# Splitting the last head group of an attention and long-convolution kernel by queries, and moving key blocks and query weights

## The chip, the core and the metric

The kernel runs on one core of a Trainium2 chip. Its engines are TensorE (PE, with its weight loads shown apart as PEld), VectorE (DVE), ScalarE (ACT), GpSimd (POOL) and SyncE (SP, which here only issues DMAs). The metric is the device time of one execution in microseconds, as the median of several runs. The profile is of one further execution; its times count from the start of its span.

## What is computed

The sequence has 2048 positions and 640 features. Two branches are mixed by a gate per position:

```
g = sigmoid((x * gate_w).sum(-1))                     # x is A_q, (2048, 640)
a = A_q * (causal_long_conv(shift(k) * v, ssm_k) + shift(k) * v * ssm_D)
q = x @ wq, 32 heads of 20;  k = x @ wk, v = x @ wv   # one key and value head for all
p = softmax(q k^T / sqrt(20)) ;  b = (p v) @ wo
out = g * a + (1 - g) * b
```

`shift` is a 4-tap filter along the sequence, and the long convolution is written with Fourier transforms. The softmax is over 2048 keys for 32 heads and 2048 queries: 134 million exponentials, which is most of the work.

## The kernel before

**Attention.** A head group is four heads times 512 queries. There are 32 groups G: four query blocks I of 512 queries with 8 groups each. The four heads sit in four strips of 32 rows, so that four score matmuls (32 rows deep) or four PV matmuls (32 columns wide) can use the array side by side. A tile is (G, j, r): group, block j of 128 keys, head r. A score tile is 128 keys by 512 queries and fills one PSUM bank.

**The score ring.** `stream` lines the tiles up and deals them into units of three and two tiles, in turn. `QK` writes a unit of three to banks 0 to 2 and one of two to banks 3 and 4; `EXP` (L1200) takes the exponential of a unit in one ScalarE instruction of 1536 or 1024 columns, into ETA or ETB; `PV` (L1241) then multiplies by the values and adds up over the key blocks in bank 6. Row 20 of the padded heads carries a bound that stands in for the maximum, and column 20 of the values is one, so that bank 6 also holds the sums. Banks 5 and 7 are left for everything else.

**Tiles on VectorE.** For the pairs (G, j) in `DVE_J` two of the four heads don't go through the ring: `DEXP` computes their exponential by a polynomial on VectorE (L1230, L1233, L1234, L1236). 94 such pairs take 188 of the 2048 tiles.

**A planner.** The instructions on each engine are not in the order of the program text. `Scheduler` plays the whole graph with costs and priorities written into the code and writes out a fixed order for each engine. PE follows the stream of score and PV matmuls, and between them it fits groups of side work (projections, shift filter, convolution, output), each into a free bank from the group's list; where nothing fits it may run filler matmuls on zeros (L1629). Each engine runs its list in order, waiting on semaphores. A changed cost, bank list or priority thus can move instructions anywhere.

**The start.** The transposed input xT is made on PE (L998). The key projection `kproj` makes four groups of 512 keys (L1017), evacuated as kT4 (L1069, L1071); the first block of 128 keys has an evacuation of its own on ScalarE. `weights2` clears the padded query weights `wq_pad` by a GpSimd memset (L983) and copies the heads into it (L986). `qproj` (L1085 and after) makes qT for some groups, squares it, sums the squares by a matmul (L1108), turns the sums into the bound (`cr`, L1114) and writes the bound into row 20 of qT by a DMA ("crow"). `kshift` loads the taps and k (a transposing DMA) and v, makes the diagonal filter matrices `kdiag` on VectorE (L1413), and runs the shift as matmuls (L1424).

**The end.** For G up to 30 `norm` copies bank 6 out, sends the sums through DRAM to spread the reciprocals, and multiplies on GpSimd (L1315). In the last query block the result goes to oT3, and `part` (L1340, L1343) adds up groups 0 to 5 of the output product ahead of time. `tail` does the last group: after its last PV it transposes bank 6 in 32x32 blocks, takes the reciprocal, multiplies, transposes back (L1353 to L1358), adds groups 6 and 7 of the output product (L1363, with warm-up matmuls L1372 beside it), and evacuates (L1387) and stores four row blocks of 128 queries.

Of the kernel before, what the change touches and what calls it, by code (L numbers as in the profile page):

```python
# [7 lines left out]
ALU = mybir.AluOpType  # L8
# [13 lines left out]
LATX = 0.12  # L22
CEX = 0.0633
LATM = {("dve", "dve"): 0.3}
# [145 lines left out]
class Scheduler:  # L170
# [278 lines left out]
    def place(self, op, e):  # L449
# [45 lines left out]
        if e == "pe":  # L495
            if op.name != "qk":
                self.rows = set()
            elif op.cont:
                self.rows.add(op.row)
            else:  # L500
                self.rows = {op.row}
        if op.name == "pv":
            self.can_fill = not op.last
            self.acc = None
        elif op.name == "acc":
            self.acc = op
# [120 lines left out]
DVE_J = [(6,), (), (4, 10), (4, 11), (2, 7, 10), (1, 4, 9, 13), (9,), (2, 7, 12), (3, 8, 13), (2, 6, 10, 14), (3, 9), (1, 4, 8, 12), (1, 2, 7, 10, 13), (8,), (1, 6, 11), (2, 7, 13), (2, 6, 10, 14), (2, 4, 7, 10, 13), (2, 6, 10, 14), (2, 9), (8,), (2, 5, 8, 11, 14), (), (2, 5, 8, 11, 14), (1, 4, 7, 10, 13), (6,), (1, 4, 7, 10, 13), (5,), (1, 4, 8, 12), (2, 5, 10, 11, 14), (1, 10, 11), (2, 8, 13)]  # L627
# [28 lines left out]
class Kernel:  # L656
# [322 lines left out]
    def weights2(self):  # L979
# [3 lines left out]
        self.pool(lambda e: e.memset(T["wq_pad"][:, :, 128:1024].bitcast(I32), 0), (), [("wq_pad", 1)], 2.1, prio=-4,  # L983
                  after=self.crow0 + [self.g.writer["kT4", 0, 128]])
        for lo, hi in ((4, 8), (8, 16), (16, 24), (24, 32)):
            self.pool(lambda e, lo=lo, hi=hi: e.tensor_copy(dst[:, :, lo:hi, 0:20], src[:, :, lo:hi, :]),  # L986
                      [("wqst", 1)], [("wq_pad", 1)], 0.75 if hi - lo == 4 else 1.5, prio=-4, name="wq_cp")
# [21 lines left out]
    def kproj(self):  # L1009
# [3 lines left out]
        for b in range(NB):  # L1013
            gr = self.group("kT", (1.9 if b == 0 else 4.0) + 0.1 * b, banks=(5, 7) if b == 0 else (7, 4, 5))
# [62 lines left out]
    def qproj(self, I, gs, prio, banks, ng):  # L1077
# [4 lines left out]
        for gl, gi in enumerate(gs):  # L1082
            gr = self.group("qp", prio, banks=banks)
            for dc in range(NDC):
# [4 lines left out]
                if dc == 0:  # L1089

                    o.deps.update(self.crow0 or ())
                    if self.crow0:
                        o.deps.add(self.g.writer["mcol"])
                    o.deps.update(self.g.readers.get(("qT", par, gi), ()))
            self.evac(gr, "dve", None, ["qup"], [("qT", par, gi)], 0.7,
# [6 lines left out]
                     [("qT", par, gi)], [("sq", gl)], c_fast(512), prio=-1500.0 if I == 0 and gs[0] == 0 else prio - 500, port=True,  # L1102
# [4 lines left out]
        for gl in range(nq):  # L1107
# [10 lines left out]
                 writes=[("qT", par, gi) for gi in gs], nbytes=4 * nq * 1024, prio=pr, name="crow", lat=1.7)  # L1118
# [15 lines left out]
    def stream(self):  # L1134
# [4 lines left out]
        for G in range(8 * NB):  # L1139
            for j in range(NSC):  # L1140
                mine = order
                if j in DVE_J[G]:
# [12 lines left out]
    def attention(self):  # L1155
# [10 lines left out]
        def score(e, bk, G, j, r):  # L1166
            return e.matmul(self.bank(bk), T["kT4"][32 * r:32 * r + 32, 128 * j:128 * j + 128],  # L1167
                            T[f"qT{G // 8 % 2}"][32 * r:32 * r + 32, G % 8, :], start=True, stop=True,
# [5 lines left out]
        def QK(n):  # L1174
            un = units[n]
            I = un[-1][0] // 8
# [8 lines left out]
            for k, (G, j, r) in enumerate(un):  # L1185
                bk = base[n % 2] + k
                o = op("pe", lambda e, bk=bk, G=G, j=j, r=r: score(e, bk, G, j, r),
                       [self.kkey(j), ("qT", G // 8 % 2, G % 8)], [("ps", bk)], 0.003 if k < len(un) - 1 else 0.216,
                       name="qk", main=True, cont=(k > 0), banks=(bk,))
                o.row = r  # L1190
                o.unit = n
                if k == 0:
# [11 lines left out]
        def DEXP(G, j):  # L1204
# [10 lines left out]
            for h, r in enumerate(rs):  # L1215
# [5 lines left out]
                self.mm(gr, lambda e, bk, r=r: score(e, bk, G, j, r), [self.kkey(j), ("qT", G // 8 % 2, G % 8)],  # L1221
# [17 lines left out]
        def PVmm(r, j, src, key, late=False, **k):  # L1239
            va = "vneg" if late else "vaug"  # L1240
            return op("pe", lambda e: e.matmul(  # L1241
                self.bank(6)[32 * r:32 * r + 32, :], T[va][:, j, :], src,
                start=(j == 0), stop=(j == NSC - 1), tile_position=(0, 32 * r)),
                [key, va, ("vaugb", j // 4)], [] if late else [("ps", 6)], name="pv", **k)

        def PV(G, j, rs, more=False):
            for k, r in enumerate(rs):
# [441 lines left out]
```

## Time and profile before

| | us |
|---|---|
| median of 3 runs (lowest to highest) | 875.41 (875.38 to 875.6) |
| the profiled execution, its own time | 876.13 |
| span of the profiled execution | 874.3 |
| start of the first exponential | 20.80 |
| last exponential begins, ends | 863.68, 864.94 |

PE's granted clock was full (1.00) in nearly the whole span. Busy time by engine over four stretches (us of the span, length, busy us and number of instructions of PE, PEld, DVE, ACT and POOL, granted clock, DMA share, GB/s):

```
24.00:50.00 26.00, 24.86 (x251) 9.70 (x252) 16.10 (x24) 25.72 (x23) 15.17 (x21) 1.00 0.72 156
300.00:600.00 300.00, 296.22 (x2717) 121.04 (x2717) 247.15 (x297) 300.00 (x266) 143.63 (x126) 1.00 0.08 24
840.00:865.00 25.00, 24.73 (x206) 10.14 (x200) 9.46 (x18) 24.93 (x23) 1.27 (x1) 1.00 0.14 45
865.00:874.30 9.30, 4.51 (x36) 2.74 (x36) 5.94 (x9) 0.00 (x0) 0.00 (x0) 0.99 0.21 73
```

How to read the profile: a row of a timeline has the start, the length, the engine, the line of the kernel, the operation, the tile written and the tile read, the count, and in brackets how long the engine was idle before it and who released it. On ScalarE an instruction's length takes in the time it stands in the engine behind its predecessor, so lengths of neighbours overlap; the pace is the distance between starts. SPq and ACTq are the issue of a DMA, not its transfer.

### The profile page before, as it was taken

To read this page: it belongs to the slowest core of one execution; us is meant where nothing else is said; L and a number is where in the kernel's file an instruction comes from. 1 tells how busy PE (TensorE), PEld (TensorE's weight loads), DVE (VectorE), ACT (ScalarE), POOL (GpSimd) and SP (SyncE) were. 2 spreads that over 40 slices of the span, in tenths; PEclk is the share of its full clock that TensorE was granted. 3 is DMA by queue.
4 is the path that set the end of the run, shared out by engine and by line. 5 is a ranking of instruction groups with operands and counts; after the bars stand their busy time and mean duration, and the time that the engine had idled before them with its cause. 6 is when DMAs were issued, how large, how long until landed. Compare 5 with 4: busy or idle time off the path is not lost.

```text
span 874.3 us, 18639 instructions
## 1 busy us (share of the span) xinstructions
PE 854.7 (98%) x8054; PEld 351.3 (40%) x8054; DVE 703.0 (80%) x906; ACT 853.4 (98%) x765; POOL 368.8 (42%) x351
## 2 busy tenths in 40 slices
PE   8999999999999999999999999999999999999997
PEld 5334424444344334444334344444444433243333
DVE  7668988895887888888789888788668788898854
ACT  6999999999999999999999999999999999999995
POOL 3572001357564434653516654436761537410000
PEclk9999999999999999999999999999999999999999
DMA  6900010001100000100000102000100000040211
GB/s 193 210 16 8 20 44 15 20 11 28 33 19 15 19 8 21 44 19 20 13 13 15 45 20 57 21 4 18 44 20 20 13 7 10 13 111 29 58 67 39
DMA packets 49713, 30.71 MB, mean 35 GB/s; under 512 B 32477, under 2 KB 45662, under 8 KB 49630
## 3 DMA queue, kind: packets, MB, share of 16 engines
q1 hardware_dynamic: 48910, 29.13, 12.3%
q8 instruction: 63, 1.03, 0.5%
q10 hardware_dynamic: 720, 0.38, 0.2%
q14 instruction: 20, 0.16, 0.1%
HBM read 17.85 MB, written 6.02 MB: 27 GB/s over the span
## 4 chain that ended last, share of the span: by engine, by line
ACT 93%; PE 6%; DVE 1%; DVEq 0%; POOL 0%; issue 0%; POOLq 0%
ACT ETA L1200 55%; ACT ETB L1200 38%; PE ps L1167 1%; PE ps L1634 1%; PE ps L998 1%; PE ps L1241 1%; PE ps L1085 1%; PE ps L1424 1%; PE ps L1629 0%; PE ps L1017 0%; PE ps L1363 0%; PE ps L1025 0%; DVE outsb L1387 0%; PE ps L1372 0%; DVE IndG L920 0%; PE ps L1108 0%
## 5 line engine op out<-in xcount | busy, mean ns | idle before, releaser
L1200 ACT ACTIVATE ETA<-ps 128x1536 bf16<-128x1536 f32 x372 | 604.7, 1625 | 2.3 <-PE ps L1167 2.3
L1200 ACT ACTIVATE ETB<-ps 128x1024 bf16<-128x1024 f32 x372 | 447.8, 1204 | 1.6 <-PE ps L1167 1.6
L1167 PE MATMUL ps<-qT,kT 32*128 32x512 bf16 x2048 | 298.6, 384 | 11.8 <-ACT ETA L1200 6.4
L1514 POOL TENSOR_TENSOR Pp<-X,K 128x512 f32<-128x512 bf16 x120 | 154.7, 1301 | 169.4 <-DVE K L1502 56.8
L1230 DVE TENSOR_SCALAR dW<-ps 128x512 f32<-128x512 f32 x188 | 129.0, 687 | 79.1 <-PE ps L1167 78.0
L1167 PEld LDWEIGHTS ps<-qT,kT 32*128 32x128 bf16 x2048 | 73.8, 91 | 249.2 <-ACT ETB L1200 126.4
L1241 PE MATMUL ps<-ETA,vaug 128*32 128x512 bf16 x1116 | 151.5, 385 | 0.3 <-ACT ETB L1200 0.3
L1241 PE MATMUL ps<-ETB,vaug 128*32 128x512 bf16 x744 | 146.9, 385 | 0.0
L1236 DVE SCALAR_TENSOR_TENSOR ETd<-dX,dW 128x1024 int16<-128x1024 f32 x94 | 133.8, 1423 | 9.7 <-PE ps L1241 9.5
L1233 DVE SCALAR_TENSOR_TENSOR dX<-dW 128x1024 f32<-128x1024 uint16 x94 | 131.3, 1397 | 1.1
L1234 DVE SCALAR_TENSOR_TENSOR dX<-dX,dW 128x1024 f32<-128x1024 f32 x94 | 126.9, 1350 | 0.4
L1514 POOL TENSOR_TENSOR AB<-Pp 128x256 bf16<-128x256 f32 x80 | 63.2, 790 | 74.4 <-DVE dX L1234 29.8
L1481 PE MATMUL ps<-ssm_kT,Tcs 128*128 128x256 bf16 x600 | 89.4, 274 | 0.0
L1547 PE MATMUL ps<-AB,Tcs 128*128 128x256 bf16 x600 | 88.5, 274 | 0.0
L1629 PE MATMUL ps<-Tcs,zeros 128*32 128x512 bf16 x1072 | 88.4, 385 | 0.1
L1481 PE MATMUL ps<-kv,Tcs 128*128 128x256 bf16 x600 | 87.5, 275 | 0.0
L1514 POOL TENSOR_TENSOR Pp<-Pp 128x512 f32<-128x512 f32 x40 | 56.8, 1419 | 40.9 <-DVE dX L1234 18.2
L1315 POOL TENSOR_TENSOR oTn<-acc,rbc 128x512 bf16<-128x512 f32 x24 | 38.2, 1593 | 76.3 <-DVE dX L1234 32.8
L1481 PEld LDWEIGHTS ps<-kv,Tcs 128*128 128x128 bf16 x600 | 49.9, 98 | 35.7 <-issue 28.7
L1547 PEld LDWEIGHTS ps<-AB,Tcs 128*128 128x128 bf16 x600 | 51.5, 98 | 31.4 <-issue 26.1
L1481 PEld LDWEIGHTS ps<-ssm_kT,Tcs 128*128 128x128 bf16 x600 | 51.0, 98 | 30.6 <-issue 23.7
L1315 POOL TENSOR_TENSOR oT<-acc,rbc 128x512 bf16<-128x512 f32 x7 | 12.1, 1733 | 81.2 <-DMA rbc<-scr_d 46.4
(132 smaller groups left out, 648.3 us busy)
## 6 DMA issues: line engine op xcount, KB each, us to landing
rbc<-scr_d SPq DMA_DIRECT2D x31, 256.0 KB
scr_o<-oTn SPq DMA_DIRECT2D x24, 128.0 KB, 1.7
xn<-in_A_q_dram SPq DMA_DIRECT2D x4, 640.0 KB, 7.7
kv<-in_A_v_dram SPq DMA_DIRECT2D x4, 640.0 KB
out_dram<-outsb SPq DMA_DIRECT2D x14, 160.0 KB, 2.2
oTp<-scr_o SPq DMA_DIRECT2D x12, 160.0 KB, 7.5
wog<-in_B_wo_dram SPq DMA_DIRECT2D x4, 200.0 KB
wo<-in_B_wo_dram SPq DMA_DIRECT2D x4, 200.0 KB, 3.3
```

The lines of the kernel that those rows point to most:

```text
L1167: return e.matmul(self.bank(bk), T["kT4"][32 * r:32 * r + 32, 128 * j:128 * j + 128], T[f"qT{G // 8 % 2}"][32 * r:32 * r + 32, G % 8, :], ...
L1200: op("act", lambda e: e.activation(et(n)[:, 0:w], self.ps[:, lo:lo + w], ACT.Exp, scale=SCALE), [("ps", base[n % 2] + k) for k in range(le ...
L1230: self.evac(gr, "dve", lambda e, bk, h=h: e.tensor_scalar(W[:, 512 * h:512 * h + 512], self.bank(bk), SCALE * LOG2E * 128.0, 128.0 * (127 ...
L1233: V(lambda e: e.scalar_tensor_tensor(X[:, :], w, DP, w, ALU.add, ALU.mult), [kW], ["dX"], c_ps(1024), **k)
L1234: V(lambda e: e.scalar_tensor_tensor(X[:, :], X[:, :], DQ, w, ALU.add, ALU.mult), [kW], ["dX"], c_ps(1024), **k)
L1236: V(lambda e: e.scalar_tensor_tensor(T[f"ETd{pe}"][:, :].bitcast(dt.int16), X[:, :], DA, W[:, :], ALU.mult, ALU.add), [kW, "dX"], [("ETd", ...
L1241: return op("pe", lambda e: e.matmul(self.bank(6)[32 * r:32 * r + 32, :], T[va][:, j, :], src, start=(j == 0), stop=(j == NSC - 1), tile_p ...
L1315: self.pool(lambda e: e.tensor_tensor(out, T["acc"][:, :], T["rbc"][:, :], ALU.mult), ["acc", "rbc"], [key], c_pool(512), prio=p, port=Tru ...
L1481: self.mm(gr, lambda e, bk, lhs=lhs, rhs=rhs, comp=comp, n=n: e.matmul(self.bank(bk, 256, 256 * comp), lhs, rhs, start=(n == 0), stop=(n = ...
L1514: f = lambda e: e.tensor_tensor(out, a, b, alu)
L1547: self.mm(gr, lambda e, bk, lhs=lhs, fc=fc, comp=comp, h=h: e.matmul(self.bank(bk, 256, 256 * h), lhs, AB[:, fc, :, comp, :], start=(fc == ...
L1629: sch.filler = [[lambda e, r=r, st=st: e.matmul(self.bank(6)[32 * r:32 * r + 32, :], self.T["zeros"][:, 0:32], self.T["Tcos"][:, 0, 0:512] ...
```

## The change

1. **The last head group in three parts.** Group 31 is worked in three passes over all keys: queries 0 to 255 (PV into bank 6), 256 to 383 (bank 5) and 384 to 511 (bank 6 again). A ring tile stays 512 columns wide: with 256 queries it holds two key blocks, with 128 queries four, each by a matmul of its own (`split`). The PV matmuls are split in the same way. After each part a new function `tail_o` does the transposes and the normalisation for that part, and the output product of the finished row blocks (three of the four) is done as side work, evacuated in halves of 320 columns and stored while the stream runs. Only the last row block is left for `tail`. The lists of banks of the late side groups take in bank 6.
2. **No VectorE tiles in the last group**, and `DVE_J` dealt out anew: 94 entries before and after, of which the two of group 31 are not used. The first two groups have none.
3. **Key blocks out of the score ring**: the groups of `kproj` may use banks 5 and 7; before, three of the four could also use bank 4.
4. **Query weights first**: the memset of `wq_pad` moves from behind the first crow DMA to behind the copies into wk4; the four copies come after the last key block; `kdiag` waits for the second of them.
5. Bookkeeping: the planner's delay from GpSimd to GpSimd, names of the qT tiles for the fences, fillers for the new banks.

In the order of instructions that the planner makes of it, the first transposes of the third input block go ahead of the first query projection, the first load of v goes ahead of the taps on SP, and the loads of the taps and of k follow.

The core of the diff:

```diff
-LATM = {("dve", "dve"): 0.3}
+LATM = {("dve", "dve"): 0.3, ("pool", "pool"): 0.0}
...
+LASTG = 31
+STAGES = ((0, 256, 6), (256, 128, 5), (384, 128, 6))
...
-        self.pool(lambda e: e.memset(T["wq_pad"][:, :, 128:1024].bitcast(I32), 0), (), [("wq_pad", 1)], 2.1, prio=-4,
-                  after=self.crow0 + [self.g.writer["kT4", 0, 128]])
+        self.pool(lambda e: e.memset(T["wq_pad"][:, :, 128:1024].bitcast(I32), 0), (), [("wq_pad", 1)], 2.0, prio=-8.9,
+                  after=[self.g.writer["wk4"]])
+        self.wq_cp = []
         for lo, hi in ((4, 8), (8, 16), (16, 24), (24, 32)):
...
+                      after=self.crow0 + [self.g.writer["kT4", NB - 1, 0]]))
...
-            gr = self.group("kT", (1.9 if b == 0 else 4.0) + 0.1 * b, banks=(5, 7) if b == 0 else (7, 4, 5))
+            gr = self.group("kT", (1.9 if b == 0 else 4.0) + 0.1 * b, banks=(5, 7))
...
-        for G in range(8 * NB):
-            for j in range(NSC):
+        for G in range(LASTG + len(STAGES)):
+            for j in range(NSC if G < LASTG else NSC * STAGES[G - LASTG][1] // 512):
                 mine = order
-                if j in DVE_J[G]:
+                if G < LASTG and j in DVE_J[G]:
...
+        def score(e, bk, G, j, r, t=0):
+            k, g = qkey(G)
+            m = split(G)
+            n, q0, jt = 512 // m, STAGES[G - LASTG][0] if m > 1 else 0, m * j + t
+            return e.matmul(self.bank(bk, n, n * t), T["kT4"][32 * r:32 * r + 32, 128 * jt:128 * jt + 128],
+                            T[k][32 * r:32 * r + 32, g, q0:q0 + n], start=True, stop=True,
                             tile_position=(32 * r, 0))
...
+                if LASTG <= G < LASTG + len(STAGES) - 1 and j == NSC // split(G) - 1:
+                    self.tail_o(G - LASTG)
...
+    def tail_o(self, h):
+        T = self.T
+        g = 7
+        q0, w, b = STAGES[h]
...
+        o = self.dve(lambda e: e.transpose(acc, self.bank(b, w)), [("ps", b)], [k["acc"]], c_ps(w), prio=p, name="tp%d" % h,
+                     after=[self.tp0] if h else ())
...
+        self.dve(lambda e: e.reciprocal(rcp, v(T["acc"])[:, :, 20]), [k["acc"]], [k["rcp"]], 0.3, prio=p, name="rcp")
+        self.dve(lambda e: e.tensor_tensor(v(T["oTn"]), v(T["acc"]), rcp.unsqueeze(2).to_broadcast([128, w // 32, 32]),
+                                           ALU.mult), [k["acc"], k["rcp"]], [k["oTn"]], c_ps(w), prio=p, port=True,
+                 name="onorm")
+        self.dve(lambda e: e.transpose(T["oT3"][:, g, q0:q0 + w], oTn), [k["oTn"]], [("oT3", g, h)],
+                 c_ps(w), prio=p, name="tp")
...
+        for ci in range(fin[0]):
...
+                gr = self.group("op2s", -800.0 + ci, banks=(7, 6, 5))
+                for g in (6, 7):
+                    self.mm(gr, lambda e, bk, g=g, ci=ci, half=half: self.tail_mm(e, self.bank(bk, HD), ci, half, g),
+                            [("oT3", g) if g < 7 else ("oT3", 7, h_of[ci]), "wog", ("part", ci)], c_mm(HD))
...
+            store(ci)
+
+        self.tail_o(len(STAGES) - 1)
...
-            ["ident", "wtap"], ["kdiag"], c_ps(2560), prio=16, port=True, name="ksh", after=[self.g.writer["kT4", NB - 1, 0]])
+            ["ident", "wtap"], ["kdiag"], c_ps(2560), prio=16, port=True, name="ksh", after=[self.g.writer["kT4", NB - 1, 0], self.wq_cp[1]])
```

## What was predicted, before the changed kernel had run

> **What bounds the kernel now.** I read the page first (busy time by engine, and the chain that ended last), then the waits of ScalarE, then the ScalarE timeline, then the stretches around each wait.
>
> From the page, sections 1 and 4, and one row of section 5:
>
> ```profile
> PE 854.7 (98%) x8054; PEld 351.3 (40%) x8054; DVE 703.0 (80%) x906; ACT 853.4 (98%) x765; POOL 368.8 (42%) x351
> ...
> ACT 93%; PE 6%; DVE 1%; DVEq 0%; POOL 0%; issue 0%; POOLq 0%
> ...
> L1200 ACT ACTIVATE ETA<-ps 128x1536 bf16<-128x1536 f32 x372 | 604.7, 1625 | 2.3 <-PE ps L1167 2.3
> ```
>
> PE shows 98% too, but part of that is filler (L1629, L1634). The chain is 93% exponentials (L1200), so ScalarE sets the time. The durations 1625 and 1204 ns include queueing. The pace is the distance from start to start in the ScalarE timeline: median 1.33 us for a 1536-wide exponential and 0.91 for a 1024-wide one, a pair in 2.24, so about 0.87 ns a column.
>
> The waits of ScalarE (us in total, times, longest), and where they lie in its timeline:
>
> ```profile
> ACT ETA L1200 <- PE ps L1167: 2.3, 2, 1.4
> ...
> ACT ETB L1200 <- PE ps L1167: 1.6, 1, 1.6
> ```
>
> ```profile
> 20.80 1.45 ACT L1200 ACTIVATE ETA<-ps 128x1536 bf16<-128x1536 f32 x1 [0.92 <-PE ps L1167]
> 23.84 1.02 ACT L1200 ACTIVATE ETB<-ps 128x1024 bf16<-128x1024 f32 x1 [1.59 <-PE ps L1167]
> ...
> 51.11 1.45 ACT L1200 ACTIVATE ETA<-ps 128x1536 bf16<-128x1536 f32 x1 [1.40 <-PE ps L1167]
> ```
>
> From 20.8 us to the last exponential's end at 864.94 there are only two real holes, 1.59 and 1.40 us. A change can win in four places: the prologue before 20.8, these holes, the number of exponential columns, and the 9.36 us from 864.94 to the end of the span, 874.30.
>
> **Hole 1, 22.2 to 23.8.** The second score unit (banks 3 and 4) starts only at 23.38. One key-block group had been put into bank 4, and its evacuation runs 22.35 to 23.30. It is late because VectorE stood still beside a GpSimd memset (timeline, VectorE and GpSimd):
>
> ```profile
> 21.31 1.97 POOL L983 MEMSET wq_pad<- 128x2240 int32 x1 [1.80 <-DVE IndG L920]
> 21.94 1.36 DVE L920 CAST IndG<-acol 128x4 bf16<-128x4 f32 x1
> 22.35 0.95 DVE L1069 TENSOR_SCALAR kT<-ps,cols 128x512 bf16<-128x512 f32 x1
> ```
>
> A four-column cast takes 0.16 us elsewhere and here ends only with the memset. The change removes both causes: key-block groups use banks 5 and 7 alone, and the memset moves to about 7.9 us, where GpSimd's own idle of 5.96 us (before 13.85) covers it. The second unit then waits only for the rest of key block 0: L1069 x2 end at 21.17, PE needs 0.39 and the handover 0.1, so it is ready at about 21.9, before the first exponential drains (20.80+1.33=22.13). The hole goes; what is late next is the third unit, behind three key-block matmuls (0.65) on PE, worth 0 to 0.15. **Taken: -1.5** (ends -1.6 and -1.0).
>
> **Hole 2, 49.6 to 51.1.** Score unit 24 is the first of head group 1, and in the order of instructions it waits for the small DMA that writes row 20 of that group's qT:
>
> ```profile
> 47.56 0.68 DVE L1114 TENSOR_SCALAR cr<-ps 8x512 int16<-8x512 int32 x1 [0.25 <-PE ps L1108]
> ...
> 48.26 0.60 SPq L679 DMA_DIRECT2D qT<-cr  x1
> ...
> 50.62 0.60 PE L1167 MATMUL ps<-qT,kT 32*128 32x512 bf16 x5
> ```
>
> From the last q2 matmul (47.14) to a ready score takes 4.0 us: matmul and cr to 48.24, DMA 2.3, score 0.5. The slot came 2.4 us after that matmul, so 1.5 were lost. In the changed order the chain has the same length, but group 0 has no tile on VectorE any more. Group 1 begins at unit 25, and its last q2 stands behind unit 23 instead of 22. Counting from the end of exponential 20: that matmul starts at +1.4 (it stands behind eight shift matmuls, a q2 and two score units), the score is ready at +5.3, the slot is at 0.91+1.33+0.91+1.33=+4.48. A hole of 0.8 stays. **Taken: -0.7** (ends -1.5, if the earlier weights move q2 further ahead, and +0.5).
>
> **Prologue.** The memset of 1.97 us may hold up two VectorE operations (0.43 and 0.28) and the first xT copy, due at 9.85. The order on PE also puts the first query projection behind 16 more transposes, so its row-20 DMA leaves SP about 0.9 later (before: 14.99). On SP the v load now goes ahead of the taps, and the taps' load waits for the last sine table; behind it stand the four transposing loads of k (SP: 17.23 to 36.3). They slip by 1 us at most, and the first shift matmuls go from unit 10 to unit 13, which covers that. On VectorE the kTr memset, which waits for that row-20 DMA, stands ahead of the reduction (17.76) that leads to the first score: 0 to 0.8. The four weight copies (0.52+3x0.85) now run unbroken after the last key block, and kdiag (2.83 on VectorE) waits for the second; ahead of unit 25 nothing on ScalarE's path needs kdiag early. **Taken: +0.2** (ends -0.3 and +1.0).
>
> **Exponential columns.** The VectorE list keeps 94 entries, but the two of the last group are now ignored: 92 pairs, 1864 tiles on ScalarE instead of 1860. In the order of instructions this is one 1536-wide exponential and one 512-wide one more: 1.34 + 0.48 (0.91 less 0.43, the step from 1536 to 1024). **+1.8**, certain.
>
> **Last head group in parts.** The same columns, but its last two parts, 32 tiles, work with 128 queries at a time: a score tile is four matmuls of 128 columns, a PV tile four. No row of before has 32-row tiles with 128 columns, and here a rule speaks against the change. The nearest row is the shift matmul, with 128-column weights and 128 columns streamed:
>
> ```profile
> 48.37 0.90 PEld L1424 LDWEIGHTS ps<-kdiag,kTr 128*128 128x128 bf16 x16 [0.42 <-DVE cr L1114]
> 48.38 1.07 PE L1424 MATMUL ps<-kdiag,kTr 128*128 128x128 bf16 x16
> ```
>
> Sixteen in about 0.9: 56 ns each, load hidden. The Trainium skill, "TensorE: Matmul & The Clock Gate", section "Back-to-back issue gap", says that in a stream of load-and-multiply pairs the sustained spacing at 128 columns is about 81 ns, since the load must be paid too, against 131 at 512: quarter matmuls cost far more than a quarter. A pair of exponentials (2.24 us) needs 20 score and 20 PV matmuls in the 128-query parts. By the rule, one after another: 40x0.081=3.2 us, plus side work 0.65 (60 output matmuls at 0.138 over the last 12.8 pairs) and about 0.45 of handovers: 4.3, so 2.1 over in each of 6.4 pairs, +13 us. By the row, with three or four tiles side by side (eight PV matmuls of 512 columns take 0.62 in the chain, not 8x0.22): 8 score steps and 5 PV steps of 0.056 to 0.08 are 0.7 to 1.05, and the sum of 1.8 to 2.15 fits under 2.24. I take the row: **+0.3** for late scores (ends 0 and +5).
>
> **The tail.** Before, after the last exponential (timeline, VectorE):
>
> ```profile
> 865.65 0.72 DVE L1353 STREAM_TRANSPOSE acc<-ps 128x512 f32<-128x512 f32 x1 [0.35 <-PE ps L1241]
> 866.40 0.25 DVE L1354 RECIPROCAL rcp<-acc 128x16 f32<-128x16 f32 x1
> 866.69 0.69 DVE L1355 TENSOR_TENSOR oTn<-acc,rcp 128x512 bf16<-128x512 f32 x1
> 867.42 0.71 DVE L1358 STREAM_TRANSPOSE oT<-oTn 128x512 bf16<-128x512 bf16 x1
> 868.73 3.26 DVE L1387 SCALAR_TENSOR_TENSOR outsb<-ps,omgf,part 128x640 bf16<-128x640 f32 x4 [0.60 <-PE ps L1363]
> ```
>
> PV 0.7, four operations 2.48, matmul 0.6, four evacuations 3.26, last store 2.3: 9.36. After: only 128 queries remain. Three of the four operations shrink to about 0.28 each (the 128x128 copy L932 takes that), the reciprocal to 0.22; with gaps 1.17: -1.3. One evacuation (0.82) instead of four: -2.45. PV, matmul and store stay. That is -3.75. Ahead of the last PV, however, PE now has a score, sixteen PV, one output and six partial-sum matmuls (about 1.9 with switches) beside the last two exponentials (1.82), and VectorE one more evacuation (0.55): +0.25. **Taken: -3.5** (ends -3.9 and -2.8). The other three stores (about 2.3 each) leave during the stream.
>
> **Sum:** -1.5 -0.7 +0.2 +1.8 +0.3 -3.5 = -3.4. The span of 874.3 becomes 870.9; that execution took 876.13, so 872.7 by its clock. Its time is 0.72 above the median of the runs shown (875.41), so the median to expect is 875.4-3.4 = **872.0**. Everywhere else VectorE tiles are dealt out anew over the groups; ScalarE's slips of 0.05 to 0.2 before a 1536-wide exponential sum to about 7 us over the whole stream, and I give their change +-1.
>
> **Rivals.**
> - *PE becomes the bound in the 128-query parts* (slower). If tiles side by side can't hide their loads, a step costs 0.15 (the 91 ns load plus 53 ns of streaming): 13x0.15+1.1=3.05 against 2.24, 0.8 in 6.4 pairs, +5.2 in place of +0.3: 876.9, and about 877.5 with the longer final PV. The gain is eaten from 0.13 a step on. For it: the rule above. Against: score loads of three tiles lie within 0.10 us of each other in the timeline. Chance 8%.
> - *Only the tail wins*: the early holes reopen elsewhere (row-20 DMA, kTr memset, taps), holes and prologue together 0: 875.4+1.8+0.3-3.5 = 874.0. Chance 20%.
> - *Both holes close and the new deal trims slips*: -1.6-1.5+0-1.0+1.8-3.7 = 869.4. Chance 17%.
>
> Forecast 55%. Its own range is 870.6 to 873.6; with the rivals the range is 869.6 to 875.0. About 0.2% (1.75 us) is what a measurement of this kernel tells from no change: faster (under 873.66) 0.78, same 0.16, slower (over 877.16) 0.06.
>
> **What would show it.** One 512-wide exponential at the end and 92 pairs of dX operations; the second exponential within 0.2 us of the first one's drain; a wait of 0 to 1.5 at unit 25; waits of ScalarE on scores under 0.1 in the last 30 us; one 640-wide evacuation after the last PV, and 5.6 to 6.2 us from the last exponential to the end. Long waits between exponentials in the last 15 us, or the first exponential over 1 us later, would prove it wrong.

## The result, and the profile after

The changed kernel takes **872.48 us** in the median of 7 runs (872.24 to 872.9); the kernel before, on the same chip, takes 875.63 (875.38 to 879.11, 7 runs). The ratio is 0.9957, with a 95% interval of 0.9944 to 0.997: faster by about 3.1 us (0.4%). The span of the profiled execution went from 874.3 to 870.7.

From the page of the changed kernel, its busy times, the shares of the chain that ended last, and the two rows of exponentials (which are now at L1227):

```profile
PE 846.3 (97%) x8157; PEld 352.7 (41%) x8177; DVE 699.7 (80%) x905; ACT 856.9 (98%) x769; POOL 380.4 (44%) x351
...
ACT 93%; PE 5%; DMA 1%; DVE 0%; SPq 0%; issue 0%
...
L1227 ACT ACTIVATE ETA<-ps 128x1536 bf16<-128x1536 f32 x373 | 607.1, 1628 | 0.6 <-PE ps L1190 0.5
L1227 ACT ACTIVATE ETB<-ps 128x1024 bf16<-128x1024 f32 (+1 forms) x373 | 449.4, 1205 | 1.3 <-PE ps L1190 1.3
```

The chain is still 93% exponentials. There are 746 of them, two more than before; the "+1 forms" is the one 512-wide exponential. ScalarE's waits for scores (engine, what it read, who released it; us in total, times, longest), and the three rows of its timeline that answer to the holes of before:

```profile
ACT ETB L1227 <- PE ps L1190: 1.3, 1, 1.3
...
ACT ETA L1227 <- PE ps L1190: 0.5, 1, 0.5
```

```profile
20.67 1.45 ACT L1227 ACTIVATE ETA<-ps 128x1536 bf16<-128x1536 f32 x1 [0.54 <-PE ps L1190]
22.02 1.02 ACT L1227 ACTIVATE ETB<-ps 128x1024 bf16<-128x1024 f32 x1
...
50.62 1.02 ACT L1227 ACTIVATE ETB<-ps 128x1024 bf16<-128x1024 f32 x1 [1.26 <-PE ps L1190]
```

The wait of 0.5 is the one ahead of the first exponential. The second one now starts 1.35 us behind the first and waits for nothing: hole 1 is gone. Hole 2 is still there, at 50.62 in place of 51.11.

The end, in the timeline of the changed kernel (PE, VectorE, ScalarE):

```profile
864.22 0.98 PE L1373 MATMUL ps<-wog,oT 128*128 128x320 bf16 x6
864.35 0.77 ACT L1227 ACTIVATE ETB<-ps 128x512 bf16<-128x512 f32 x1
...
865.24 0.55 DVE L1376 SCALAR_TENSOR_TENSOR part<-ps,omgf,kv 128x320 f32<-128x320 f32 x1 [0.26 <-PE ps L1373]
...
865.71 0.31 DVE L1389 STREAM_TRANSPOSE acc<-ps 128x128 f32<-128x128 f32 x1
...
866.05 0.18 DVE L1393 RECIPROCAL rcp<-acc 128x4 f32<-128x4 f32 x1
...
866.26 0.29 DVE L1394 TENSOR_TENSOR oTn<-acc,rcp 128x128 bf16<-128x128 f32 x1
866.59 0.31 DVE L1397 STREAM_TRANSPOSE oT<-oTn 128x128 bf16<-128x128 bf16 x1
...
867.44 0.88 DVE L1458 SCALAR_TENSOR_TENSOR outsb<-ps,omgf,part 128x640 bf16<-128x640 f32 x1 [0.54 <-PE ps L1403]
868.35 0.35 ACTq L687 DMA_DIRECT2D out_dram<-outsb  x1
```

Where four operations took 0.25 to 0.72 each and four evacuations 3.26, there are now four of 0.18 to 0.31 and one evacuation of 0.88. The last partial sum of the output product (L1376) stands just ahead of the transpose. The last exponential ends at 865.12, and 5.58 us are left; before, it was 9.36.

The account, term by term, from the profiled execution of each kernel. "Over" is the distance from one exponential's start to the next, less the usual pace.

| term | predicted | measured | from |
|---|---|---|---|
| first exponential | +0.2 | -0.13 | 20.80 to 20.67 |
| hole 1 | -1.5 | -1.69 | first to second start, 3.04 to 1.35 |
| hole 2 | -0.7 | +0.09 | over: 1.54 (2.45 less 0.91) to 1.63 (2.97 less 1.34) |
| exponential columns | +1.8 | +1.82 | 1.34 + 0.48, counted at the usual pace |
| late scores in the last group | +0.3 | 0 | no wait of ScalarE after 50.62 |
| other slips | 0 (+-1) | +0.09 | rest, to the last exponential's end |
| tail | -3.5 | -3.78 | 9.36 to 5.58 |
| sum | -3.4 | -3.60 | 874.3 to 870.7 |

The first term is within what one execution varies from the next: four kernels with the same start (changed, dve94, move25, parts4, below) have their first exponential at 20.38 to 20.80.

### The profile page after: what moved, and what is told of

Same layout as the page of the kernel before. It is cut to its first block, busy times and chain, and to the rows that moved or that the text cites. A ratio compares the mean times of both kernels' runs of the same rounds, so it can differ in the third digit from the quotient of the medians.

```text
span 870.7 us, 18888 instructions
## 1 busy us (share of the span) xinstructions
PE 846.3 (97%) x8157; PEld 352.7 (41%) x8177; DVE 699.7 (80%) x905; ACT 856.9 (98%) x769; POOL 380.4 (44%) x351
## 4 chain that ended last, share of the span: by engine, by line
ACT 93%; PE 5%; DMA 1%; DVE 0%; SPq 0%; issue 0%
ACT ETA L1227 55%; ACT ETB L1227 38%; PE ps L1190 1%; DMA xn<-in_A_q_dram 1%; PE ps L1373 1%; PE ps L1095 1%; PE ps L1268 1%; PE ps L1494 1%; PE ps L1403 0%; PE ps L1008 0%; SPq L687 0%; PE ps L1035 0%; PE ps L1027 0%; PE ps L1118 0%; DVE outsb L1458 0%
## 5 line engine op out<-in xcount | busy, mean ns | idle before, releaser
L1227 ACT ACTIVATE ETA<-ps 128x1536 bf16<-128x1536 f32 x373 | 607.1, 1628 | 0.6 <-PE ps L1190 0.5
L1227 ACT ACTIVATE ETB<-ps 128x1024 bf16<-128x1024 f32 (+1 forms) x373 | 449.4, 1205 | 1.3 <-PE ps L1190 1.3
L1190 PE MATMUL ps<-qT,kT 32*128 32x512 bf16 (+2 forms) x2176 | 301.0, 372 | 14.5 <-ACT ETA L1227 8.0
L1584 POOL TENSOR_TENSOR Pp<-X,K 128x512 f32<-128x512 bf16 x120 | 164.0, 1383 | 146.5 <-DVE K L1572 48.9
L1268 PE MATMUL ps<-ETA,vaug 128*32 128x512 bf16 (+2 forms) x1196 | 153.9, 371 | 0.0
L1268 PE MATMUL ps<-ETB,vaug 128*32 128x512 bf16 (+2 forms) x796 | 148.5, 371 | 0.0
L1260 DVE SCALAR_TENSOR_TENSOR dX<-dW 128x1024 f32<-128x1024 uint16 x92 | 128.5, 1397 | 1.0
L1584 POOL TENSOR_TENSOR AB<-Pp 128x256 bf16<-128x256 f32 x80 | 66.1, 826 | 68.3 <-DVE dX L1260 24.6
L1551 PE MATMUL ps<-ssm_kT,Tcs 128*128 128x256 bf16 x600 | 89.0, 275 | 0.0
L1551 PE MATMUL ps<-kv,Tcs 128*128 128x256 bf16 x600 | 87.4, 275 | 0.1
L1699 PE MATMUL ps<-Tcs,zeros 128*32 128x512 bf16 x944 | 77.9, 385 | 0.7 <-DVE acc L1336 0.5
L1584 POOL TENSOR_TENSOR Pp<-Pp 128x512 f32<-128x512 f32 x40 | 53.9, 1348 | 39.3 <-DVE dX L1261 19.1
L1551 PEld LDWEIGHTS ps<-ssm_kT,Tcs 128*128 128x128 bf16 x600 | 50.6, 97 | 32.5 <-issue 25.9
L1551 PEld LDWEIGHTS ps<-kv,Tcs 128*128 128x128 bf16 x600 | 49.7, 97 | 34.2 <-issue 27.5
L1348 POOL TENSOR_TENSOR oT<-acc,rbc 128x512 bf16<-128x512 f32 x7 | 8.9, 1272 | 85.3 <-DMA rbc<-scr_d 60.3
```

Source lines behind the costliest of these rows:

```text
L1190: return e.matmul(self.bank(bk, n, n * t), T["kT4"][32 * r:32 * r + 32, 128 * jt:128 * jt + 128], T[k][32 * r:32 * r + 32, g, q0:q0 + n], ...
L1227: op("act", lambda e: e.activation(et(n)[:, 0:w], self.ps[:, lo:lo + w], ACT.Exp, scale=SCALE), [("ps", base[n % 2] + k) for k in range(le ...
L1260: V(lambda e: e.scalar_tensor_tensor(X[:, :], w, DP, w, ALU.add, ALU.mult), [kW], ["dX"], c_ps(1024), **k)
L1268: return op("pe", lambda e: e.matmul(self.bank(b, n)[32 * r:32 * r + 32, :], T[va][:, j, :], src, start=(j == 0), stop=(j == NSC - 1), til ...
L1348: self.pool(lambda e: e.tensor_tensor(out, T["acc"][:, :], T["rbc"][:, :], ALU.mult), ["acc", "rbc"], [key], c_pool(512), prio=p, port=Tru ...
L1551: self.mm(gr, lambda e, bk, lhs=lhs, rhs=rhs, comp=comp, n=n: e.matmul(self.bank(bk, 256, 256 * comp), lhs, rhs, start=(n == 0), stop=(n = ...
```

## The experiments

There were twelve runs, two of them of one kernel. Times are medians, ratios are to the kernel before, run beside it. Four numbers are read from each profile: the start of the first exponential, the end of the last, the **tail** from there to the end of the span, and the start of the last matmul of the inverse transform, where the convolution on PE ends.

| kernel | time | ratio (95%) | first exp. starts | last exp. ends | tail | last inverse |
|---|---|---|---|---|---|---|
| before | 875.63 | 1 | 20.80 | 864.94 | 9.4 | 823.2 |
| after | 872.48 | 0.9957 (0.9944 to 0.997) | 20.67 | 865.12 | 5.6 | 820.2 |
| early_only | 888.07 | 1.0129 (1.0112 to 1.0146) | 20.43 | 867.61 | 18.0 | 846.2 |
| tail_only | 882.81 | 1.0068 (1.0051 to 1.0085) | 21.14 | 868.95 | 12.2 | 836.1 |
| q1_alone | 887.79 | 1.0128 (1.0107 to 1.0149) | 20.36 | 865.04 | 20.5 | 849.9 |
| parts4 | 874.47 | 0.9965 (0.9945 to 0.9985) | 20.80 | 865.26 | 7.4 | 820.4 |
| move25 | 872.87 | 0.9965 (0.9951 to 0.9979) | 20.48 | 864.98 | 5.5 | 820.1 |
| old_deal | 876.77 | 1.0011 (1.0003 to 1.0018) | 20.75 | 869.28 | 5.5 | 819.7 |
| early_newdeal | 880.91 | 1.0054 (1.0034 to 1.0074) | 21.16 | 864.00 | 15.6 | 833.3 |
| bank4_timed (= bank4_back) | 871.95 | 0.9951 (0.9939 to 0.9964) | 20.69 | 864.49 | 5.5 | 818.7 |
| bank4_94 | 882.13 | 1.007 (1.0058 to 1.0083) | 20.39 | 863.59 | 16.7 | 839.7 |
| dve94 | 885.12 | 1.0101 (1.0087 to 1.0115) | 20.38 | 875.94 | 5.5 | 815.7 |
| memset_late | 874.3 (one run) | - | 20.22 | 864.84 | 7.4 | 824.5 |

The last two columns go together. Among the kernels with the last group in parts (all but before, early_only and early_newdeal) the tail is 5.5 to 5.6 where the inverse transform ends by 820.2, 7.4 at 820.4 (parts4, which has one part more to finish) and 824.5, and 12.2, 16.7 and 20.5 at 836.1, 839.7 and 849.9. In the kernels with the last group in one piece it is 9.4, 15.6 and 18.0 at 823.2, 833.3 and 846.2. This is a comparison of plans that differ in more than this one place.

### The two halves of the change, one at a time

**early_only**: the kernel before with the early edits alone (the bank list of `kproj`, the memset, the weight copies, `kdiag`'s wait).

```diff
-            gr = self.group("kT", (1.9 if b == 0 else 4.0) + 0.1 * b, banks=(5, 7) if b == 0 else (7, 4, 5))
+            gr = self.group("kT", (1.9 if b == 0 else 4.0) + 0.1 * b, banks=(5, 7))
...
-        self.pool(lambda e: e.memset(T["wq_pad"][:, :, 128:1024].bitcast(I32), 0), (), [("wq_pad", 1)], 2.1, prio=-4,
-                  after=self.crow0 + [self.g.writer["kT4", 0, 128]])
+        self.pool(lambda e: e.memset(T["wq_pad"][:, :, 128:1024].bitcast(I32), 0), (), [("wq_pad", 1)], 2.0, prio=-8.9,
+                  after=[self.g.writer["wk4"]])
...
+                      after=self.crow0 + [self.g.writer["kT4", NB - 1, 0]]))
```

> The kernel before, with the key blocks on banks 5 and 7, the early memset, the later weight copies and the wait of kdiag alone; last head group and VectorE tiles as before. Sum theory: hole 1 goes (start to start of the first two exponentials 3.04 to about 1.35), the first exponential within 0.3 of 20.8, hole 2 stays near 1.5, tail 9.4: span about 872.6, 1.7 under before. Rival (the planner's new order of the whole stream gives it, not the first hole): span under 871.5 or over 873.5.

**tail_only**: the changed kernel with these same edits undone. The new deal of VectorE tiles and the planner's delay thus count with this half.

> The changed kernel with the early edits undone (bank 4 allowed, late memset, copies and kdiag as before), the last group in three parts kept. Sum theory: hole 1 is back with 1.6, the end after the last exponential stays 5.6, one and a third exponentials more than before (+1.8): span 874.3+1.8-3.8 = 872.3. Rival (the parts only pay together with the early edits): span 874 or more.

Both are slower than the kernel before, so the change is not the sum of two gains that each stand alone. In early_only hole 1 is gone (21.77 is 1.34 behind 20.43), but hole 2 grew to 5.48, and at the end the output product is left over. Its ScalarE timeline, and from its list of instructions by line the first and last start of the output product (duration in ns lowest/median/highest, then the two starts; L1579 and L1342 are L1647 and L1373 of the changed kernel):

```profile
53.26 1.45 ACT L1202 ACTIVATE ETA<-ps 128x1536 bf16<-128x1536 f32 x1 [5.48 <-PE ps L1169]
```

```profile
L1579 PE MATMUL ps<-wo,oTp x120: 299/299/311, 823.2 to 868.8; 128*128 128x320 bf16 x120
...
L1342 PE MATMUL ps<-wog,oT x48: 299/299/310, 869.0 to 875.8; 128*128 128x320 bf16 x48
```

In the changed kernel L1647 runs from 790.8 to 846.3, under the exponentials; here its last matmul starts 1.2 us after the last one has ended, and the partial sums come behind it. tail_only has the same fault in a smaller size: the last of its partial sums (L1372) starts at 875.4, 6.4 us after the last exponential has ended, and hole 1 is back (21.14 to 24.19, 3.05). Both sum theories on record were thus wrong by 9 to 13 us of span, and both rivals right.

### Which edit closed hole 1

**bank4_back** and **bank4_timed** are the same kernel (871.8 in one run, then five runs): the changed kernel with the old bank list of `kproj`, so the memset early and bank 4 allowed again.

> The changed kernel with bank 4 allowed for key blocks again; memset still early. If bank 4 is the cause of hole 1: the first two exponentials start 2 us or more apart. If the memset is the cause: 1.35 to 1.5 apart. The rest of the stream is planned anew and may leave side work at the end.

> The kernel after with one edit undone (key-block group 0 may use banks 5 and 7, the others 7, 4 and 5, as before), now timed over five rounds; a single look gave a span of 870.0. Theory: once the memset is early, the bank rule costs the first pair of exponentials 0.4 to 0.6 us and is otherwise no more than a new plan; a median of 871.4 to 872.6, so not told apart from after (872.5). Rival: the bank rule is what closes hole 1 and a part of the gain rests on it; then 873.5 or more.

**memset_late**: the bank rule kept, the memset and only it put back (its priority too, from -8.9 to -4).

```diff
-                  after=[self.g.writer["wk4"]])
+                  after=self.crow0 + [self.g.writer["kT4", 0, 128]])
```

> The kernel after with the query weights' memset put back to its later place (behind the first row-20 transfer and the first key block), the bank rule kept. If the memset is the larger part of hole 1, the second exponential again starts 0.8 us or more late (2.2 us or more behind the first, after: 1.35); if the bank was, it starts about 1.4 to 1.9 us behind the first. The rest of the plan may change, so only this place is read.

The ScalarE timeline of bank4_timed, and that of memset_late with its VectorE and GpSimd rows:

```profile
20.69 1.45 ACT L1227 ACTIVATE ETA<-ps 128x1536 bf16<-128x1536 f32 x1 [0.92 <-PE ps L1190]
22.60 1.02 ACT L1227 ACTIVATE ETB<-ps 128x1024 bf16<-128x1024 f32 x1 [0.46 <-PE ps L1190]
```

```profile
20.22 1.45 ACT L1227 ACTIVATE ETA<-ps 128x1536 bf16<-128x1536 f32 x1 [0.55 <-PE ps L1190]
...
20.89 2.34 DVE L928 CAST IndG<-acol 128x4 bf16<-128x4 f32 x3
21.03 1.97 POOL L991 MEMSET wq_pad<- 128x2240 int32 x1 [1.72 <-DVE kT L1079]
...
21.57 1.02 ACT L1227 ACTIVATE ETB<-ps 128x1024 bf16<-128x1024 f32 x1
```

The four cases, as the distance from the first to the second exponential: bank 4 and late memset 3.04 (before; 3.05 in tail_only), bank 4 and early memset 1.91, bank rule and late memset 1.35, both 1.35 (after). So each edit works at this place, and the bank rule alone is enough. The 1.91 lies between the two bands expected for bank4_back; what is left of the hole there is PE's order, in which seven key-block matmuls (from 20.52, for 1.69) stand ahead of the second unit. In memset_late VectorE stands beside the memset as it did before: three casts of four columns take 2.34 us together, and end at 23.23. But no score waits for them any more, since the second unit's bank doesn't have to be evacuated first. The first of the two readings on record for memset_late (the memset is the larger part) is wrong; the stall of VectorE was real, and the bank made it count.

The bank rule does one thing more, which no one had counted. From the start of the evacuation that the first score waits for (L1071 before, L1081 after) to that score it takes 0.42 to 0.43 in all nine kernels with the rule, and 0.79 to 0.80 in all five runs without it, where PE is still in a longer row of key-block matmuls. Before and after:

```profile
18.48 1.89 PE L1017 MATMUL ps<-xT,wk 128*128 128x512 bf16 x8
...
19.51 0.37 ACT L1071 ACTIVATE kT<-ps,cols 128x128 bf16<-128x128 f32 x1 [0.26 <-DVE cols L1061]
...
20.30 0.39 PE L1167 MATMUL ps<-qT,kT 32*128 32x512 bf16 x3
```

```profile
18.73 1.24 PE L1027 MATMUL ps<-xT,wk 128*128 128x512 bf16 x5
...
19.76 0.37 ACT L1081 ACTIVATE kT<-ps,cols 128x128 bf16<-128x128 f32 x1 [0.26 <-DVE cols L1071]
...
20.18 0.39 PE L1190 MATMUL ps<-qT,kT 32*128 32x512 bf16 x3 [0.20 <-ACT kT L1081]
```

As a whole bank4_timed is not told apart from the changed kernel (0.9951 against 0.9957). It loses 0.56 at hole 1, but has no hole 2, since its plan came out differently there. So the gain of the whole change does not rest on the bank rule. memset_late has no hole 2 either, and a wait of 1.10 at 855.21; its time, a single run, is not compared.

### What keeps hole 2 open

The timeline of the changed kernel around the wait:

```profile
45.77 0.38 PE L1118 MATMUL ps<-sq,IndG 128*8 128x512 bf16 x1
...
46.40 0.38 PE L1118 MATMUL ps<-sq,IndG 128*8 128x512 bf16 x1
...
46.94 0.67 DVE L1124 TENSOR_SCALAR cr<-ps 8x512 int16<-8x512 int32 x1
...
47.64 0.60 SPq L687 DMA_DIRECT2D qT<-cr  x1
...
49.68 0.56 PE L1494 MATMUL ps<-kdiag,kTr 128*128 128x128 bf16 x7
...
50.16 0.60 PE L1190 MATMUL ps<-qT,kT 32*128 32x512 bf16 x5
```

The chain has the links that were seen before: last q2 matmul, `cr`, the small DMA, score. Two things are late in it. The last q2 starts at 46.40, which is 1.90 after exponential 20 gives way to the next (44.50); the prediction had counted 1.4. And ahead of the score on PE stand seven shift matmuls (L1494), which wait for an evacuation that ends at 49.49.

**move25** takes the second away: after the planner, the score matmuls of unit 25 are put ahead of those seven on PE.

```diff
+        qk = [o for o in pe if o.name == "qk" and o.unit == 25]
...
+        while pe[a - 1].name == "kc":
+            a -= 1
...
+            seq[at:at] = qk
```

> The changed kernel with one swap in the fixed order of PE: the two score matmuls of unit 25 go ahead of the seven shift matmuls that stand before them (which wait for an evacuation on VectorE). Nothing else moves. Theory A (hole 2 is the row-20 DMA alone): the wait before exponential 25 stays at 1.26. Theory AB (the DMA lands at about 49.5 and the shift matmuls then add 0.6): the wait falls to 0.6 to 0.8 and the span to about 870.1. Theory B (side work alone): the wait falls under 0.2, span about 869.5.

From its ScalarE timeline:

```profile
50.04 1.02 ACT L1227 ACTIVATE ETB<-ps 128x1024 bf16<-128x1024 f32 x1 [0.86 <-PE ps L1190]
...
53.66 1.45 ACT L1227 ACTIVATE ETA<-ps 128x1536 bf16<-128x1536 f32 x1 [0.34 <-PE ps L1190]
```

The wait fell from 1.26 to 0.86 (over: 1.63 to 1.24), a little above the 0.6 to 0.8 that was expected for two causes together, and a new wait of 0.34 (over 0.46) came 3.6 us later, as the shift matmuls that were passed over had to be done then. From the first exponential to the last nothing changed (843.68 us between their starts in the one, 843.73 in the other). So 0.4 of the hole is side work, and the rest is the chain over the DMA. Putting off side work that PE must do anyway gave nothing back.

**q1_alone** attacks the first: group 1 gets a query projection of its own, ahead of the others.

```diff
-        for b, gs in enumerate(([0], [1, 2], [3, 4], [5, 6], [7])):
+        for b, gs in enumerate(([0], [1], [2, 3], [4, 5], [6, 7])):
```

> The changed kernel with the query projections of block 0 dealt out as group 0, 1, 2-3, 4-5, 6-7 instead of 0, 1-2, 3-4, 5-6, 7. Theory A for hole 2 (late is the chain projection, q2, cr, row-20 DMA of group 1, for which two projections have to be done): its q2 comes some five units earlier, the wait at unit 25 goes, span about 869.4, 1.3 under the changed kernel. Theory B (late is the side work that stands ahead of the score unit on PE, a shift group that waits for its evacuation): the wait stays within 0.4 of 1.3, span 870.3 to 870.9.

Hole 2 is gone in it altogether, and the time is 15 us worse. Its list by line shows why:

```profile
L1647 PE MATMUL ps<-wo,oTp x120: 299/299/311, 830.2 to 869.3; 128*128 128x320 bf16 x120
```

The output product starts at 830.2 in place of 790.8, since the convolution it needs ended later: the last matmul of the inverse transform lies at 849.9, in the changed kernel at 820.2. The stream of exponentials itself ended at the same place (865.04). What was won at 50 us was paid at the end, many times over. The convolution and this product are tied in the code: the product's weights and inputs (`wo`, `oTp`) lie in the memory of the spectra, and its evacuation (L1650) adds the convolution's result. In q1_alone 16 of its 24 evacuations come after the last inverse transform.

The other traces show what the rest of hole 2 hangs on. In the kernels whose group 1 begins at unit 25 (dve94 and parts4 are as the changed kernel there, bank4_94 as bank4_timed), the place of the last q2 matmul, counted from the end of exponential 20, goes with what is over:

| kernel | last q2 | exponential 25 starts, after that q2 | over |
|---|---|---|---|
| q1_alone | -2.48 | 7.12 | 0 |
| bank4_timed | -0.5 | 4.9 | 0 |
| early_newdeal | 0.81 | 4.06 | 0.30 |
| memset_late | 0.93 | 4.01 | 0.25 |
| tail_only | 1.7 | 4.6 | 1.86 |
| changed kernel | 1.90 | 4.22 | 1.63 |
| move25 | 1.90 | 3.83 | 1.24 |

Where anything is over, the exponential starts 3.8 to 4.6 after the last q2, the chain of cr, DMA and score. The slot of exponential 25 is 4.48 after the end of exponential 20, so as an estimate the hole closes when the last q2 starts by about 0.5 (4.48 less some 4.0). From the timeline of memset_late:

```profile
45.00 0.38 PE L1118 MATMUL ps<-sq,IndG 128*8 128x512 bf16 x1
...
49.01 1.02 ACT L1227 ACTIVATE ETB<-ps 128x1024 bf16<-128x1024 f32 x1
```

### Whether 128-query parts are dear for PE

**parts4** works the last group in four parts of 128 queries, so that all 64 tiles and not half of them go through quarter matmuls (in it the last group gets no filler matmuls, and the order of the new transposes is fixed for one part more).

```diff
-STAGES = ((0, 256, 6), (256, 128, 5), (384, 128, 6))
+STAGES = ((0, 128, 6), (128, 128, 5), (256, 128, 6), (384, 128, 5))
```

> The changed kernel with the last head group in four parts of 128 queries (no 256-query part; no filler matmuls in the last group). Doubles the 128-query matmuls: 64 ring tiles instead of 32. If a step of 128 columns costs about 56 ns side by side (row), scores are on time and the end after the last exponential stays 5.6: span within 0.5 of 870.7. If matmuls of 128 columns cost about 81 ns one after another, PE falls behind by 2 us in each of 6.4 more pairs: span over 880.

ScalarE never waits in its last 70 us, and the last exponential ends at 865.26, 0.14 from the changed kernel's. The 2.0 us it is slower lie in the tail: one partial sum still runs on PE after the last exponential (six matmuls from 866.24), and the normalisation stands behind its evacuation on VectorE. The expectation of a tail of 5.6 was missed for that reason, and not for the cost of a step:

```profile
867.26 0.55 DVE L1379 SCALAR_TENSOR_TENSOR part<-ps,omgf,kv 128x320 f32<-128x320 f32 x1 [0.35 <-PE ps L1376]
867.73 0.28 DVE L1397 TENSOR_TENSOR oTn<-acc,rcp 128x128 bf16<-128x128 f32 x1
```

The step itself is read in the changed kernel's timeline, in the second part:

```profile
853.46 0.40 PE L1190 MATMUL ps<-qT,kT 32*128 32x128 bf16 x12
...
854.70 0.23 PE L1268 MATMUL ps<-ETA,vaug 128*32 128x128 bf16 x2
...
854.76 0.22 PE L1268 MATMUL ps<-ETA,vaug 128*32 128x128 bf16 x2
...
854.82 0.22 PE L1268 MATMUL ps<-ETA,vaug 128*32 128x128 bf16 x2
...
854.87 0.22 PE L1268 MATMUL ps<-ETA,vaug 128*32 128x128 bf16 x2
```

Twelve score matmuls of 128 columns, three at a time side by side, take 0.40 from the first start to the last end, hardly more than the 0.39 of three with 512 columns. The PV matmuls follow each other in steps of 0.05 to 0.06, four in each step (the ETB rows between are left out).

### The price of the exponential columns, and the deal to VectorE

**old_deal**: the changed kernel with the `DVE_J` of before (91 pairs count). **early_newdeal**: early_only with the new list (all 94 count).

> The changed kernel with the list of VectorE tiles of the kernel before (its three pairs of group 31 are not used: 91 pairs, two more tiles on ScalarE). If the new deal is only a small matter of slips: +0.9 for the two tiles and +-1, span 870.6 to 872.6. If the deal is what lets the convolution and output work end with the stream (as the two kernels that kept one half of the change suggest): last exponential within 2 us of 866, but side work left over after it, span over 876.

> The kernel before with the early edits and also the new list of VectorE tiles (94 pairs, the two of group 31 used), last head group in one piece. If the deal was what early_only lacked: span 872.6 (874.3 less 1.7), tail after the last exponential 9.4. If side work is late with any list but the one a plan was fitted to: tail over 11, span over 874.

**dve94** and **bank4_94**: a third column block on VectorE in each of two groups, so 94 pairs and 1860 tiles on ScalarE, in the changed kernel and in bank4_back. As entries of the list:

```diff
-DVE_J[18] = (4, 11)
-DVE_J[23] = (1, 5, 11)
+DVE_J[18] = (2, 7, 12)
+DVE_J[23] = (1, 5, 9, 13)
```

> As bank4_timed, and two more column blocks of the exponential are dealt to VectorE (a third one in groups 18 and 23 of the list), so that ScalarE has 1860 tiles as before the change and not 1864. Theory of the sum: one 1536-wide and one 512-wide exponential fewer, 1.34+0.48 = 1.8 us: a median near 870.2. Rival, from the runs so far: a new deal re-orders the side work, and what is left of it after the last exponential decides; then the time is off this by several us in either direction, and the tail is longer than 5.6 us.

> The kernel after with the same two column blocks more on VectorE and nothing else. Theory of the sum: 872.5-1.8 = 870.7. Rival: side work left over, a tail of more than 5.6 us and 873 or more.

In old_deal hole 2 is 3.28 us, with more waits of 0.68 at 771.11 and 0.23 at 773.70; no side work is left over. These waits (over: 3.50, 1.06 and 0.34, less the 1.63 of the changed kernel) and 0.9 for its two more tiles on ScalarE account for the 4.16 by which its last exponential ends later. The expectation that the new deal is there to let the side work end before the stream was thus wrong for it. With the new list early_only loses most of hole 2 (over 0.3), gets a wait of 0.91 at 612.96, and keeps a tail of 15.6.

The sum said that two column blocks more on VectorE save 1.8 us. bank4_94 does have a shorter stream (its last exponential ends 0.90 earlier than in bank4_timed, after a start 0.30 earlier and with a new wait of 0.72 at 557.62), and then a tail of 16.7 us: partial sums (L1373) run up to 874.5. dve94 keeps the tail of 5.5, which neither reading on record had, and has one wait of over ten microseconds instead. Its timeline there (PE, VectorE, ScalarE):

```profile
715.95 1.63 DVE L1263 SCALAR_TENSOR_TENSOR ETd<-dX,dW 128x1024 int16<-128x1024 f32 x1
...
717.63 0.39 PE L1268 MATMUL ps<-ETd,vneg 128*32 128x512 bf16 x2 [0.50 <-DVE ETd L1263]
...
718.39 0.61 PE L1190 MATMUL ps<-qT,kT 32*128 32x512 bf16 x6
```

```profile
718.85 1.02 ACT L1227 ACTIVATE ETB<-ps 128x1024 bf16<-128x1024 f32 x1 [10.33 <-PE ps L1190]
```

Counting tiles, this exponential holds the seventh and eighth tile of group 26, three groups behind the last one that was dealt more. The PV of a VectorE tile (vneg) waits for its polynomial, which ends at 717.58; on PE the next unit's scores stand behind that PV; so ScalarE stands still although its own work is ready to be made. In the ten microseconds before, VectorE did the convolution's evacuations and the polynomial in turn, with 1.70 of idleness on convolution matmuls of PE (L1551) between. Here the wait is named in the trace; why the planner let it grow there was not tried.

## Why the prediction was right, and where it was not

The forecast of 872.0 came within 0.5 us of the measured 872.48, inside its own range, for mostly the reasons it gave.

- **The tail, -3.5**: right, measured -3.78. The four operations from transpose to transpose gave -1.29 (-1.3 counted), the evacuation -2.38 (-2.45 counted). The partial sum that the prediction put beside the last exponentials did run there, but the 0.25 allowed for it did not appear: from the last exponential's end to the first transpose it took 0.59, before 0.71.
- **Hole 1, -1.5**: right, measured -1.69. The four cases above show both named causes at work. The prediction took both to be removed and did not say that one was enough.
- **Exponential columns, +1.8, "certain"**: right as a count, +1.82. But the experiments show it isn't a price at which the columns can be bought back: taking them away made two kernels slower by 10 to 13 us.
- **The last head group in parts, +0.3**: right in its choice, measured 0. The row (56 ns in the shift matmuls) was weighed against the rule of the Trainium skill, "TensorE: Matmul & The Clock Gate", section "Back-to-back issue gap" (about 81 ns a pair at 128 columns; the 81 ns in the expectation of parts4 are the same). The trace gives 55 to 57 ns a step, each of three or four tiles side by side, and parts4 with twice as many such tiles had no late score. The measurement decides for the row: in this kernel quarter matmuls on separate strips cost a quarter.
- **Prologue, +0.2**: measured -0.13, inside the ends given, but partly by luck. The first crow DMA did slip (14.99 to 15.60), and the evacuation that the first score waits for started 0.25 later (19.51 to 19.76). The bank rule took 0.37 back on PE, a term that the prediction had nowhere.
- **Hole 2, -0.7: the step that failed**, measured +0.09, inside its wide ends (-1.5 to +0.5). The prediction said "a hole of 0.8 stays"; over 1.63 stayed. Its working had the last q2 at +1.4 behind exponential 20, and it came at +1.90; and it took the score to follow the DMA at once, where seven shift matmuls stood ahead of it, for 0.4. The order on PE was read as far as the q2 and not on to the score. The miss of 0.8 did not show in the sum, since the other terms came out better than counted by 0.2 (hole 1), 0.3 (tail), 0.3 (late scores) and 0.3 (first exponential). That the total came so near is in this part luck.
- **The rival "only the tail wins"** (874.0) is out, since hole 1 closed. **Both holes close and the new deal trims slips** (869.4) is out, since hole 2 stayed and the slips came to +0.09. The rival with **PE as the bound** is out by the step of 56 ns. What no rival had was what the runs showed most clearly: the left-over of the side work. early_only, q1_alone and bank4_94 each win at the place they aim at, and end 6 to 12 us later than the kernel before, with tails of 16.7 to 20.5 us. The slip of "+-1" that the prediction allowed for the new plan was, in these neighbours of the change, up to 15 us. That the changed kernel's own plan left nothing over is seen in its trace (the last L1373 starts at 864.9); its order of instructions on PE, with nothing of the output product behind the last PV but the last row block, hints at it in advance.
- **The signs** that were to show it came out: 92 pairs of dX operations, one 512-wide exponential at the end, the second exponential with the first one's drain, no late score, 5.58 us at the end (5.6 to 6.2 was said). The wait of 1.26 at unit 25 lies in the "0 to 1.5" given for it, a band too wide to tell a hole that closes from one that stays.

What stays open: why one small edit makes the planner finish the convolution 30 us later (q1_alone) and another doesn't. The runs show that it happens and where it is paid, not which cost or priority tips it. Of the kernels that ran, none is faster than the changed one by more than the intervals. Hole 2 with the q2 alone moved ahead, and all else held in place, was not tried; the table above compares whole plans.

## What to carry to other kernels

When one engine is busy for 98% of the span, look for a second chain of nearly the same length behind it (here the convolution and output product on PE and VectorE): an edit that shortens the first only helps if the second still ends with it, so check where the last side work stands before adding up local gains. Read the order of a latency chain to its last link, including what stands ahead of that link on its engine. And where a wait has two causes, as with a stalled evacuation and a bank that needs it, removing the dependence was enough here (1.35 with the memset still late), and speeding up the evacuation alone was not (1.91).

## What the runs showed of the hardware

- Small matmuls on separate strips of the array: a score tile of four 128-column matmuls costs PE hardly more than one of 512 columns (0.40 against 0.39 us for three tiles), although each loads its own weights (a median of 91 ns a load for the scores and 93 for PV, overlapping in the trace).
- A GpSimd memset of 2240 int32 a partition held up small VectorE operations wherever it was put: three casts of four columns took 2.34 us beside it in memset_late, against 0.58 in the changed kernel. In its early place an operation of 514 columns took 2.15 us beside it, against 0.43 in the kernel before:

```profile
7.63 2.12 POOL L991 MEMSET wq_pad<- 128x2240 int32 x1
7.87 2.15 DVE L908 TENSOR_SCALAR tprod<-tprod 128x514 int32<-128x514 int32 x1
```

- The small DMA from `cr` to qT (eight rows of 512 for a pair of groups) takes about two microseconds from its issue to the score that reads it: 2.13 in move25, 2.42 in memset_late and 2.48 in early_newdeal, all without shift matmuls in between, and 2.52 in the changed kernel with them.
